# A written instruction order made anew: GpSimd held behind VectorE's integer steps in the first stages, and new lists for the rest

## The chip, the cores and the metric

The kernel runs on one NeuronCore of one Trainium2 chip. The core has a matrix engine (TensorE, PE in the profile), three engines for elementwise work (VectorE = DVE, ScalarE = ACT, GpSimd = POOL) and a sync engine (SP) that here only issues transfers. The metric is the device time of one execution in microseconds (us), lower is better; times are medians over runs.

## The reference

Two blocks, one behind the other. The first is attention through a small set of inducing points: 4 batches of 12,416 rows with 128 channels, 32 inducing rows.

```python
def mab(q, kv):
    s = scale * (q @ kv.transpose(0, 2, 1))
    s = s - s.max(-1, keepdims=True)
    a = np.exp(s)
    a /= a.sum(-1, keepdims=True) + 1e-09
    return a @ kv
h = mab(I, x)                  # 32 rows attend to all of x
attn_out = mab(x, h)           # each row of x attends to the 32 rows h
```

The second takes all 49,664 rows through an RMS norm and a SwiGLU network with an inner width of 1536:

```python
xn = x / np.sqrt(np.mean(x * x, -1, keepdims=True) + 1e-06) * rms_g
g = xn @ w_gate
out = (g / (1.0 + np.exp(-g)) * (xn @ w_val)) @ w_out
```

The three weight matrices arrive as 64-bit floats, and the chip has to make 32-bit floats of them.

## The kernel before, in words

The second attention and the gate and value products are folded together: per batch the kernel computes h, multiplies it into `w_gate` and `w_val`, and keeps the result as stacks `sg` and `sv`. A row of x then needs its 32 normalised attention weights, split into a high and a low half and laid out by four transfers as a moving operand `a` (`gather`, L633 to L647), and one product each with a 128-wide slice of `sg` and `sv`.

**Units and blocks.** A batch has 25 units of up to 512 rows, 100 in all; a unit has 12 blocks, one for each 128 of the inner width. A block is a gate product (L709), a silu on ScalarE (L719), a value product (L737), the product of both on VectorE (L751), and the way through `w_out` to the unit's output bank. That way has three kinds, chosen per block by the letters of the list `sorts`:

- P: one product in plain fp32 (`project_plain`, L807), which reads u and `wo` as they are.
- S: u stays in a PSUM bank; ScalarE makes a high part (L764), VectorE the low part (L770), GpSimd a sum (L815), and TensorE runs three fp32r products (L795, L796, L807).
- D: u lies in SBUF; ScalarE makes the high part (L761, L783), GpSimd the low part and the sum (L777, L815), then the same three products.

So a P costs more on TensorE and less on the other three; S and D spread the other work differently over VectorE, ScalarE and GpSimd.

**What sets the order.** Nothing is scheduled by a compiler: every engine gets its instructions in the order in which the Python code emits them, and semaphores make an engine wait for data. For the first stages, up to the first gate products, the order is the string `ORDER` in `first()`, beside `BANKS`, `WORKERS` and `OUTPUTS` for the buffers. Its words are steps: `t` turns a strip of x by TensorE, `c` copies it out (its last letter is the engine: A, V or G), `s` makes scores, `m` takes them out with their maximum, `e` exponentials, `r` turns them by VectorE, `h` sums. `th` and `hT` end the first attention. Then come, in three parts k = 0, 1, 2 of the first 512 rows, `sc`, `T`, `rm`, `sub`, `ex` (scores, turn, row maximum, subtraction, exponential), `ta`, `sq`, `zm`, `sm`, `mm`, `rt`, `ap` (the norm; `rt` is a power on GpSimd, L1066), `tb`, `hi`, `lo` (the halves), and `sdh`, `sdl`, `sdm`, `cpa`, `cpb`, which lay out the first two units' operands by products with a selection matrix (L1088). `silu` loads ScalarE's table. `w4` are four products of the identity with itself into a bank that nobody reads (`warm`, L158).

Between them stand the steps that make 32-bit weights (`rounding`): for chunk `ic`, `p` and `u` (L231, L244) cut out exponent and mantissa as integers on VectorE, `P` and `U` (L209, L211) turn them into numbers, `g` and `l` (L253, L259) put sign and low word in, `j` (L265) is the product of both parts on GpSimd, `q` sends it off.

After `first()` the rest follows a second set of lists: `program` gives one letter per step, a dot standing for the next of 879 numbered steps in `taken` (strip loads L111, row loads L104, turns, norms, weight steps and so on), and `banks`, `workers`, `outputs`, `holders`, `picks` and `sorts` give each its bank, buffer or kind. Both sets are outputs of a planner that searches with its own costs; only the lists stand in the kernel.

In the loop over `program`, a GpSimd instruction that is emitted next after one of the weight steps `power`, `upper`, `sign` or `lower` gets a wait for that VectorE instruction. `first()` has no such rule.

Strip loads (`load_channels`) bring 32 channels of a later batch's rows each, in short pieces; they go through the same SP queue as the gathers and the stores.

Of the kernel before, what the change touches and what calls it, by code (L numbers as in the profile page):

```python
# [18 lines left out]
P = 128  # L19
# [4 lines left out]
def kernel(  # L24
# [10 lines left out]
    nc = tc.nc  # L35
# [236 lines left out]
    turns, works, outs, factors = [], [], [], []  # L272

# [600 lines left out]
    for s in (1, 2, 0, *range(3, NS)):  # L874
# [8 lines left out]
        0123410234012340123401234012304132041320413024301  # L883
    """
    WORKERS = "012021"
    OUTPUTS = "01010"
    ORDER = """
        open w11 t13 t11 t12 t10 c11A w1 t21 c12A t23 c13V c10V t20 c21A s1 c20V t01 c23V c01A m1 t00 c00A t22 t03 t02
        c22A s2 c02A c03V s0 m2 t31 m0 own0 t33 c31V c33V t43 mB0 nb0 t30 c30V c43A e2 t32 c32V t40 c40V t41 t53 e1 c41A
        r2 t42 r1 t60 c53A p00 u00 e0 t51 c60A c42A ls0 t52 r0 t50 s3 c51A s6 c50A s4 c52A p10 P10A m3 P00A s5 m6 p20  # L890
        P20A h0 m4 m5 own1 mB1 own2 mB2 g00 U00A nb1 l00 e3 nb2 u20 h1 h2 r3 h3 e5 r5 e4 j00 e6 least r4 ls1 h5 ls2
# [10 lines left out]
    def first():  # L902
# [343 lines left out]
    def seams():  # L1246
# [13 lines left out]
        5672340156372450721456701425140571240715420745127450172407512510752317052317024537032407263742746043267304234073  # L1260
        4270327053127305127031251512450126401526140526041245143624532757364735263456735745146517507654107641754055172457
        3571725742135724130725412354615267526471260541072467043764162106714625014725437240732413072103271403716207365127
        6351726513267136364716376471630714306217420761405726450145102614264350264032520754302434750324102475146506267467
        0526470357620165073126507261576507610576501463154634165462526531246534127651675042607456270452706534253761374623
        4726314672312470612764125714257162517462714751467104360146703476014721367306327652062763765230176501201327041270
        2731047230276346734267432643572453670524605246104561462105640216412354362514516521467562317546230152304624254302
        4675204375230170412032731243710421013641263416536253421632451637167457614164501765124705140512521054314523045301
        2754207356047235275204352407310723420473407624073062753046705435637306350160576132751037501347531740537415074316
        5074150714570124502674150415301673107160731531602761057140520645165065241046045314350434145101305147320154703427
        6073657043574657403643517654752732674723546725340673241062703620172610732617036172517602407645067562405764350243  # L1270
# [288 lines left out]
```

## Time and profile before

| | |
|---|---|
| median of 3 runs | 1473.55 us (1472.82 to 1476.4) |
| the profiled execution's own time | 1473.84 us |
| its span in the trace | 1472.1 us |
| busy: PE / DVE / POOL / ACT | 1462.6 / 1427.8 / 1374.5 / 1305.7 us |
| granted TensorE clock, mean | 0.999 |
| first gate product (L709) starts at | 45.05 us |
| PE busy from 64 us to 1467.1 us | 1403.09 of 1403.10 us |
| DVE busy in the same stretch | 1374.70 us |

Times in the trace count from the span's start. A line of the timeline gives start, length, engine, code line, operation, what is written and read, shape and count, and in brackets the idle time before it with what ended it. A name with "ld" (PEld) is a weight load, one with "q" a queue that issues. TensorE's matmuls overlap: a row's length is longer than its distance to the next start, so costs on TensorE are read from distances. A granted clock of 1.00 is full speed, 0.50 half.

### The profile page before, as it was taken

Reading aid. Unit: us, or ns where it says so; the run is one execution under the profiler, and the core shown is the slowest. Engines: PE = TensorE matmul, PEld = TensorE weight load, DVE = VectorE, ACT = ScalarE, POOL = GpSimd, SP = SyncE. Lnnn points to the kernel's source line nnn. Section 1 sums busy time; section 2 is a strip of 40 time slices with the busy share of each in tenths; the row PEclk is TensorE's granted clock in tenths of the full one; section 3 lists DMA queues with packets and bytes.
Section 4 is the critical chain, followed back from the end, with each engine's and each line's share of the span. In section 5 each row is a group of like instructions: output and inputs, shape, how many; then the busy total and the mean of one; then the engine's idle time right before and its main releaser. Section 6 shows DMA issues by size and latency. Waiting matters only on the chain.

```text
span 1472.1 us, 26044 instructions
## 1 busy us (share of the span) xinstructions
PE 1462.6 (99%) x7303; PEld 1105.9 (75%) x7303; DVE 1427.8 (97%) x2483; ACT 1305.7 (89%) x2604; POOL 1374.5 (93%) x1212
## 2 busy tenths in 40 slices
PE   9999999999999999999999999999999999999998
PEld 7566777867777777786777777787777777777787
DVE  7999999999999999999999999999999999999998
ACT  5798899889998889998989898998998899989997
POOL 1499998999999999899999999899999999999998
PEclk9999999999999999999999999999999999999999
DMA  7754323557434131455655212263322112122122
GB/s 282 148 102 101 68 42 75 114 128 137 84 66 87 29 70 39 104 122 107 127 89 108 51 36 47 50 130 94 67 57 47 33 37 44 37 40 40 38 41 35
DMA packets 391904, 116.02 MB, mean 79 GB/s; under 512 B 365648, under 2 KB 371280, under 8 KB 389200
## 3 DMA queue, kind: packets, MB, share of 16 engines
q1 hardware_dynamic: 391168, 114.28, 37.7%
q8 instruction: 58, 0.95, 0.3%
q14 instruction: 86, 0.70, 0.2%
q10 hardware_dynamic: 592, 0.08, 0.0%
HBM read 53.95 MB, written 27.00 MB: 55 GB/s over the span
## 4 chain that ended last, share of the span: by engine, by line
PE 96%; DVE 1%; DMA 1%; issue 0%; SPq 0%; POOL 0%; ACT 0%; DVEq 0%
PE gv L807 32%; PE gv L709 17%; PE gv L737 17%; PE gv L795 12%; PE gv L796 12%; PE gv L316 3%; PE gv L369 1%; DMA xn<-in_x_dram 1%; PE gv L563 1%; PE gv L457 0%; PE gv L978 0%; SPq L104 0%; DVE o L259 0%; DVE u L751 0%; PE gv L934 0%
## 5 line engine op out<-in xcount | busy, mean ns | idle before, releaser
L719 ACT ACTIVATE silu<-gv 128x512 f32<-128x512 f32 (+2 forms) x1200 | 675.0, 591 | 81.1 <-PE gv L709 64.6
L815 POOL TENSOR_TENSOR xn<-xn,xn 128x512 fp32r<-128x512 f32 (+2 forms) x489 | 604.8, 1252 | 15.2 <-PE gv L796 10.3
L709 PE MATMUL gv<-a,sg 128*128 128x512 f32 (+2 forms) x1188 | 481.6, 432 | 0.0
L737 PE MATMUL gv<-a,sv 128*128 128x512 f32 (+2 forms) x1188 | 449.7, 411 | 0.0
L751 DVE TENSOR_TENSOR gv<-silu,gv 128x512 f32<-128x512 f32 (+2 forms) x653 | 429.0, 676 | 7.5 <-ACT silu L719 3.6
L764 ACT ACTIVATE xn<-gv 128x512 fp32r<-128x512 f32 (+1 forms) x630 | 368.7, 597 | 31.9 <-DVE gv L751 26.0
L751 DVE TENSOR_TENSOR u<-silu,gv 128x512 f32<-128x512 f32 (+2 forms) x547 | 347.6, 653 | 7.5 <-PE gv L737 3.9
L807 PE MATMUL gv<-u,wo 128*128 128x512 f32 (+2 forms) x718 | 352.1, 575 | 0.2 <-POOL wo L265 0.2
L770 DVE SCALAR_TENSOR_TENSOR xn<-xn,gv 128x512 fp32r<-128x512 f32 (+2 forms) x508 | 332.0, 664 | 7.1 <-ACT xn L764 4.8
L709 PEld LDWEIGHTS gv<-a,sg 128*128 128x128 f32 x1188 | 224.4, 190 | 100.0 <-issue 30.5
L737 PEld LDWEIGHTS gv<-a,sv 128*128 128x128 f32 x1188 | 223.8, 189 | 90.3 <-issue 21.1
L815 POOL TENSOR_TENSOR xn<-xn 128x512 fp32r<-128x512 f32 (+2 forms) x185 | 232.5, 1260 | 7.5 <-PE gv L796 4.7
L777 POOL TENSOR_TENSOR xn<-u,xn 128x512 fp32r<-128x512 f32 (+2 forms) x166 | 204.5, 1237 | 12.7 <-ACT xn L761 11.4
L815 POOL TENSOR_TENSOR u<-xn,u 128x512 fp32r<-128x512 f32 (+1 forms) x143 | 180.0, 1267 | 0.8 <-PE gv L796 0.7
L795 PE MATMUL gv<-xn,xn 128*128 128x512 f32 (+2 forms) x447 | 169.7, 380 | 0.0
L807 PEld LDWEIGHTS gv<-u,wo 128*128 128x128 f32 x718 | 133.8, 190 | 26.9 <-issue 9.5
L807 PE MATMUL gv<-xn,xn 128*128 128x512 f32 (+2 forms) x372 | 139.5, 386 | 0.0
L796 PE MATMUL gv<-xn,xn 128*128 128x512 f32 (+2 forms) x372 | 139.1, 374 | 0.0
L795 PE MATMUL gv<-xn,more 128*128 128x512 f32 (+2 forms) x341 | 131.3, 385 | 0.0
L761 ACT ACTIVATE xn<-u 128x512 fp32r<-128x512 f32 (+2 forms) x187 | 115.6, 619 | 9.6 <-DVE u L751 8.1
L783 ACT ACTIVATE xn<-xn 128x512 fp32r<-128x512 f32 (+2 forms) x187 | 116.3, 628 | 7.0 <-POOL xn L777 5.8
L807 PE MATMUL gv<-xn,more 128*128 128x512 f32 (+2 forms) x286 | 110.8, 392 | 0.0
(235 smaller groups left out, 1840.5 us busy)
## 6 DMA issues: line engine op xcount, KB each, us to landing
out_dram<-o SPq DMA_DIRECT2D x320, 64.0 KB, 2.0
xT<-in_x_dram SPq DMA_DIRECT2D x60, 256.0 KB, 4.4
xn<-in_x_dram SPq DMA_DIRECT2D x60, 256.0 KB, 5.1
a<-hi SPq DMA_DIRECT2D x152, 64.0 KB, 2.0
a<-lo SPq DMA_DIRECT2D x152, 64.0 KB, 2.0
xn<-in_x_dram SPq DMA_DIRECT2D x5, 1024.0 KB, 9.3
xn<-w SPq DMA_DIRECT2D x18, 256.0 KB, 4.1
out_dram<-o SPq DMA_DIRECT2D x64, 60.0 KB, 2.0
```

The source lines that it names most:

```text
L709: nc.tensor.matmul(g[:, 0:T], stacks[b][0][:, ts(j, P)], halves_in_turn(one["a"][:, 0:T]), start=True, stop=True)
L719: nc.scalar.activation(sl[:, 0:T], gates.pop(n)[:, 0:T], AF.Silu)
L737: nc.tensor.matmul(v[:, 0:T], stacks[b][1][:, ts(j, P)], halves_in_turn(one["a"][:, 0:T]), start=True, stop=True)
L751: nc.vector.tensor_tensor(out=to, in0=sl[:, 0:T], in1=v[:, 0:T], op=ALU.mult)
L764: nc.scalar.activation(hi, t["u"], AF.Copy, scale=-(1.0 - 2.0 ** -13) * 2.0 ** -12)
L770: nc.vector.scalar_tensor_tensor(out=t["lo"], in0=t["hi"].bitcast(F32), scalar=4096.0, in1=t["u"], op0=ALU.mult, op1=ALU.add)
L777: nc.gpsimd.tensor_tensor(out=t["lo"], in0=t["u"], in1=t["hi"].bitcast(F32), op=ALU.subtract)
L783: nc.scalar.activation(t["hi"], t["hi"].bitcast(F32), AF.Copy, scale=-(2.0 ** -12))
L795: nc.tensor.matmul(to, weight_of(0, j), halves_in_turn(t["hi"]), start=not one["q"], stop=False)
L796: nc.tensor.matmul(to, weight_of(1, j), halves_in_turn(t["lo"]), start=False, stop=last)
L807: nc.tensor.matmul(to.rearrange("p (n h) -> p h n", h=2) if step2 else to, lhsT, rhs, start=one["left"] == NJ, stop=one["left"] == 1)
L815: nc.gpsimd.tensor_tensor(out=t["lo"], in0=t["hi"].bitcast(F32), in1=t["lo"].bitcast(F32), op=ALU.add)
```

## The change

Three things are edited.

1. The rule that makes GpSimd wait becomes a function `in_turn`, used by `first()` as well. After a step in `locks` (the integer steps `p`, `u`, `g`, `l`, and those `P`, `U`, `fr` that are given to VectorE), its last instruction is held; the next step that ends in a GpSimd instruction gets a wait on it at its first instruction.
2. `ORDER` and `BANKS` are new. Among other things one strip copy fewer is on VectorE, `sub0` goes from GpSimd to VectorE and `sub2` the other way, `ap1` goes to VectorE, `lo0` and `lo1` go from VectorE to GpSimd, `silu` stands ahead of `hi0`, and the unread products are 23 in all (22 before), eight of them right ahead of `sdh0` and six where eleven stood at the start.
3. All lists of the rest are new. By `sorts` there are 354 P, 662 S and 184 D (359, 653 and 188 before). In rows of 512, 480 and 256, P goes from 267, 71, 21 to 266, 69, 19, and S from 542, 97, 14 to 548, 94, 20. Steps and shapes are otherwise the same.

```diff
+    held = []
+
+    def in_turn(step, args, lock):
+        made = len(nc.cur_bb.bb.instructions)
+        step(*args)
+        new = nc.cur_bb.bb.instructions[made:]
+        if lock:
+            held[:] = new[-1:]
+        elif held and new and new[-1].engine == mybir.EngineType.Pool:
+            tc.add_manual_dep(new[0], held.pop().name, mybir.DependencyInfo(mybir.DependencyClass.Sync, mybir.DependencyReason.DATA),
+                              reason="no two at the shared port")
...
     ORDER = """
...
-        share shared tl r6 g10 spl rl U20A h4 q00 hs0A frA th0 u10 hs1A h6 l20 g20 U10A l10 hs2A th1 th2 hTA w2 sc0 p11
-        hgA sqh gc T0 rm0 sc1 j20 T1 sub0G ex0 rm1 sub1G sc2 T2 ta0 ex1 u11 ta1 st0 sq0 zm0 stc0 U11A q20 j10 q10 P11A
-        sm0 mm0V w1 sq1 rt0 rm2 zm1 sub2V sm1 ex2 mm1V w2 st1 stc1 ap0V tb0 hi0 low0 w4 sdh0 rt1 lo0V low1 sdl0 ap1G
-        sdm0 silu tb1 hi1 cpb0A p01 cpa0V lo1V P01A w1 sdh1 sdm1 sdl1 cpb1A cpa1A u01 U01V
...
+        shared r6 tl p20 p01 hs0A spl P10A hs1A h5 rl frA th0 P20A u20 g10 q00 l10 U20A l20 h6 hs2A g20 th1 w1 th2 hTA
+        w2 sc0 T0 hgA P01A sc1 T1 rm0 sqh j20 gc sc2 rm1 sub1G sub0V T2 ex0 ta0 ex1 ta1 st0 rm2 j10 w1 sq0 stc0 zm0 sm0
+        sub2G mm0V sq1 ex2 zm1 rt0 sm1 mm1V low0 ap0V tb0 silu hi0 rt1 ap1V st1 stc1 tb1 lo0G hi1 w8 sdh0 q20 w1 sdl0
+        p11 sdm0 lo1G cpa0A sdh1 low1 cpb0A P11A w1 sdm1 u01 u11 q10 cpb1A U01V sdl1 cpa1A U11V
     """
...
+        locks = {f"{key}{i}{c}{by}" for i, c in chunks for key, by in (*zip("pugl", ("",) * 4), ("P", "V"), ("U", "V"))} | {"frV"}
         for name in ORDER.split():
-            do[name]()
+            in_turn(do[name], (), name in locks)
...
-    held = None
     alone = {id(one[name]) for one in weight.values() for name in ("power", "upper", "sign", "lower")}
     for name in "".join(program.split()):
-        made = len(nc.cur_bb.bb.instructions)
         step, args = micros[int(next(taken))] if name == "." else (do[name], ())
-        step(*args)
-        one = nc.cur_bb.bb.instructions[-1]
-        if id(step) in alone:
-            held = one
-        elif held is not None and one.engine == mybir.EngineType.Pool and len(nc.cur_bb.bb.instructions) > made:
-            tc.add_manual_dep(one, held.name, mybir.DependencyInfo(mybir.DependencyClass.Sync, mybir.DependencyReason.DATA),
-                              reason="no two at the shared port")
-            held = None
+        in_turn(step, args, id(step) in alone)
```

More of the change, by code (lines that the diff above doesn't have):

```diff
@@ L1284 @@
-        2407563240762347017
+        5674130256174302653024631602314062310426304162403164026143614302614076214076241036421635260135215603251032512034
+        5704571042751407523071207310273610276037231627361237013125317247315472150732457125321627536751671236153076513750
+        7453451401743052173021735203105705635761760345701547341725702754751047624752370250240542764207560274602174603241
+        0217413720546130173051354731703105340571245743673741534367317451267345173461540635613465036154025360432473604727
@@ L1285 @@
+        3241063247012640162
     """
     workers = """
-        20120201201201022012102210210211212012100120120102012012020120120
+        20120102102102010120120201201201201201212120120102011021010210210
     """
@@ new lines @@
+        AAAAAAAAAAAAABAAAAAABAABAAAAAAABAAAAAAAAAABAACAACABAAAAAABABAAAAAAABAAAAAAAAAAAAAAAAAAAABAAAAAAAABAAAAAAAABAAAAA
+        ABAAAAAABAAAAAAAAABAAAAABAAAAABAAAAAAAAABAAAAABAAAAAAABAAAAAAAAAAAAAAAAAAAAAAAAAAAAABAAAAAAAAAABAAAAABAAAAAAAAAA
+        AABAAAAAAABAAAAAAABABAAABABBAAABAAAAAAAAAACAAAAAAAAAAAAAAAAAAABAAAAAAAAAAABAAAAAAAAAAAAAAAAABAAAAAAAAAAAAAABAAAA
+        AAAAAAAAAAAAABAAAAAAABAAAAAAAAABABAAAAAAAAAAAAAAAAAAAAAAAAAAAAAAAAAAAAAAAAAAAAAAAAAABAAAAAAABAAAABAAAAAABAAAAAAA
+        AAAAABAAAAAAAAABAAAAAAAAAAAAAAAAAAAAAAAAABAAAAAAABAAAAABAAABAAAA
```

395 lines of the change are left out of this document (193 added, 202 removed), and 60 rows, old and new, of the table taken.

## The prediction

> **What bounds the kernel now.** I read the totals first, then busy time by stretch, then TensorE's waits.
>
> ```profile
> span 1472.1 us, 26044 instructions
> PE 1462.6 (99%) x7303; PEld 1105.9 (75%) x7303; DVE 1427.8 (97%) x2483; ACT 1305.7 (89%) x2604; POOL 1374.5 (93%) x1212
> ```
> ```profile
> core 0: us, PE busy (x) PEld busy (x) DVE busy (x) ACT busy (x) POOL busy (x), PEclk, DMA share, GB/s
> 38.38:41.79 3.41, 3.03 (x18) 2.32 (x18) 3.24 (x12) 2.77 (x6) 2.15 (x3) 1.00 0.84 245
> 41.79:45.20 3.41, 2.57 (x18) 2.14 (x18) 3.26 (x9) 2.59 (x6) 0.30 (x1) 1.00 1.05 166
> 45.20:48.62 3.42, 3.42 (x13) 2.21 (x15) 3.42 (x7) 2.76 (x7) 0.27 (x2) 0.50 0.34 55
> 48.62:64.00 15.38, 15.19 (x54) 7.58 (x55) 13.77 (x26) 10.07 (x19) 7.56 (x6) 1.00 0.81 162
> 64.00:1467.10 1403.10, 1403.09 (x6772) 1064.72 (x6770) 1374.70 (x2351) 1266.45 (x2520) 1355.89 (x1179) 1.00 0.36 72
> ```
> ```profile
> PE gv L158 <- POOL ident masks.py:199: 1.3, 1, 1.3
> ...
> PE gv L807 <- POOL wo L265: 0.2, 1, 0.2
> ```
>
> From 64 us to the last product TensorE is never idle, and VectorE is idle for 28.4 us of 1403.1. The list of TensorE's waits has six rows that add up to 4.2 us (first and last shown), and all lie ahead of 64 us. So a change can pay in two ways: the first 45 us, whose length goes straight into the end, or less work on TensorE. A stall behind 64 us can hardly be removed, but it can be added. The third row of the stretches is the odd one: for 3.42 us the granted clock is 0.50, right where the first gate products run.
>
> **The first stages, the wait at GpSimd.** The timeline shows what the new wait is aimed at:
>
> ```profile
> 31.39 0.41 DVE L244 TENSOR_SCALAR o<-sc 128x512 int32<-128x512 int32 x1
> 31.71 0.68 DVE L259 SCALAR_TENSOR_TENSOR o<-sc,o 128x512 f32<-128x512 uint32 x1
> 33.07 1.27 POOL L265 TENSOR_TENSOR wo<-o,we 128x512 f32<-128x512 f32 x1 [3.80 <-DVE we L253]
> 33.10 1.79 DVE L259 SCALAR_TENSOR_TENSOR o<-sc,o 128x512 f32<-128x512 uint32 x1
> 36.75 1.27 POOL L265 TENSOR_TENSOR silu<-o,we 128x512 f32<-128x512 f32 x1
> 36.93 1.37 DVE L244 TENSOR_SCALAR o<-sv 128x512 int32<-128x512 int32 x1
> ```
>
> The same steps take 0.68 and 0.41 us alone, 1.79 and 1.37 us when a GpSimd product started just ahead of them. So two collisions hold VectorE for 1.11 and 0.96 us. What stands behind them:
>
> ```profile
> 34.24 0.43 PE L1025 MATMUL gv<-xT,hT 128*32 128x128 f32 x8
> 35.15 0.30 DVE L1028 STREAM_TRANSPOSE sc<-gv 128x128 f32<-128x128 f32 x1
> 37.06 0.49 PE L1049 MATMUL gv<-eT,gram 128*128 128x128 f32 x2 [0.21 <-DVE eT L1045]
> 38.45 0.25 DVE L1053 TENSOR_TENSOR eT<-gv,eT 128x128 f32<-128x128 f32 x1
> 39.33 1.04 POOL L1066 TENSOR_TENSOR rs<-ms,mhalf 128x4 f32<-128x4 f32 x1 [1.31 <-DVE ms L1062]
> 41.09 0.69 DVE L486 TENSOR_TENSOR sg<-gv,sg 64x512 fp32r<-64x512 f32 x1
> 41.09 0.30 ACT L1078 CAST hi<-eT 128x128 fp32r<-128x128 f32 x1
> 41.41 1.28 ACT L1107 ACT_TABLE_LOAD   x1
> 41.82 0.42 DVE L1084 TENSOR_TENSOR lo<-eT,hi 128x128 fp32r<-128x128 f32 x1
> 43.34 0.30 ACT L1078 CAST hi<-eT 128x128 fp32r<-128x128 f32 x1 [0.43 <-DVE eT L1073]
> 45.05 1.00 PE L709 MATMUL gv<-a,sg 128*128 128x512 f32 x2
> ```
>
> - *First turn of scores (35.15).* The scores are there at 34.67, and the turn waits for VectorE: at least 0.4 us comes back. One strip copy fewer and one earlier `r` take up to 0.7 us more off VectorE, but other chains feed hT as well: 0 to 1.1, and I take **0.6**, the near end being what the row shows.
> - *From that turn to the power (39.33), 4.18 us.* The square is done at 37.55, and its product (38.45) sits behind the stretched step of 36.93: 0.85 back. The new order puts `sub0` on VectorE behind T1, rm0 and rm1, and a weight step (0.73) more on ScalarE ahead of `ex0`: 0.2 given. Net 0.65.
> - *Power to second half (43.34).* `low0` (0.69) no longer stands between `hi0` and `lo0`; `ap1` and `tb1` no longer wait behind L486. Against it, the table load (1.28) is now ahead of `hi0`; laid out with these lengths it ends 0.3 us too late. The wait brings one cost of its own: `lo1` on GpSimd is held by `p11` on VectorE (L231, 0.4 us), of which 0.3 lies beside `hi1`. Laid end to end, the first gate product comes 8.1 us behind the first turn where it came 9.9 us behind it. The sum of small steps is sure only by half, so 0.6 to 2.4, and I take **1.7**.
>
> Queued behind GpSimd's new waits are only `sub1` and `sub2` (L1036): each join in question needs a late integer step of its own anyway. Six unread products where eleven stood lengthen nothing; they run while the first strips land.
>
> **The clock.** Eight products run in the stretch at 0.50. Two distances from later, at full speed, and the cost of a plain product:
>
> ```profile
> 607.47 0.38 PE L795 MATMUL gv<-xn,more 128*128 128x512 f32 x1
> 607.68 0.38 PE L796 MATMUL gv<-xn,more 128*128 128x512 f32 x1
> 608.55 1.02 PE L807 MATMUL gv<-u,wo 128*128 128x512 f32 x2
> 609.62 0.38 PE L795 MATMUL gv<-xn,xn 128*128 128x512 f32 x1
> ```
>
> A full-speed fp32r product takes 0.215 us, so half speed costs 3.42/2 = 1.7 us. It follows 3.41 us with little on TensorE (sixteen selections at about 0.06 and four unread passes, some 1.1 us, though its row says 2.57, since lengths overlap). The new order puts eight unread products (two passes at 0.11 each: 1.75 us) into that gap. The 38.38 stretch, with 3.03 in its row, was not followed by a slow one. A gap with 1.75 us of passes more should resemble it: I take **1.7**; the ends are 0 and 1.7, since I don't know what fill suffices.
>
> By the Trainium skill, TensorE: Matmul & The Clock Gate (The HAM clock gate), the watch window of some 3.4 us runs freely and does not start with the kernel; the 3.41 us here agree. By that rule the order cannot place the window, and this term would be 0 or 1.7 by chance.
>
> **TensorE's work behind that.** Between 608.55 and 609.62 stand one plain product and one value product of 0.215: a P is 0.86, three fp32r products are 0.65. Five P less and five triples more: 512 rows 1 × 0.21, 480 rows 2 × 0.20, 256 rows 2 × 0.11, so **0.8** off.
>
> ```profile
> L770 DVE SCALAR_TENSOR_TENSOR xn<-xn,gv 128x512 fp32r<-128x512 f32 (+2 forms) x508 | 332.0, 664 | 7.1 <-ACT xn L764 4.8
> ```
>
> Nine S more (by length 6, −3, 6) put 6 × 0.66 − 3 × 0.62 + 6 × 0.4, about 4.5 us, on VectorE; its 28.4 us of idle time hide it, at nothing. With that cover gone it is 4.5.
>
> **The new lists.** TensorE's order is as dense, so I take 0 for stalls; the ends: −3 (no more than the few tenths between rows could give) and, above, late gathers:
>
> ```profile
> 110.44 0.57 SPq L647 DMA_DIRECT2D a<-hi  x1
> 112.96 0.58 SPq L647 DMA_DIRECT2D a<-lo  x1
> 115.20 0.59 PE L709 MATMUL gv<-a,sg 128*128 128x512 f32 x2
> DMA to landing us min/median/max: 2.0/2.3/3.2
> xT<-in_x_dram SPq DMA_DIRECT2D x60, 256.0 KB, 4.4
> ```
>
> The fourth transfer of this gather, issued at 112.96, lands at 114.96 at best, 0.24 us ahead of the gate product that reads it. Strip loads take 4.4 where a gather takes about 2. A rule that lets gathers behind them come later cannot gain where nothing waits; it can only keep such a margin.
>
> **Sum.** 0.6 + 1.7 + 1.7 + 0.8 = 4.8 off the profiled execution's 1473.84 (its span 1472.1 and 1.7 around it): 1469.0. That execution was 0.3 above the median, which gives 1468.7; I say 1468.9.
>
> **The rivals.**
>
> - *The slow window comes all the same*, elsewhere or in the same place: 1468.9 + 1.7 = 1470.6. For it: I don't know the fill that suffices.
> - *The earlier start is eaten.* VectorE still has weight steps between 48.62 and 64 us, and it is busy for 13.77 of 15.38 us there, a tenth from full; if those steps hold the first units, the 2.3 us of the first stages are lost, and with the clock unhealed all but 0.8: 1471 to 1473. Against it: the row still has 1.6 us free.
> - *The shared path hits other steps.* A GpSimd join slows not just integer steps: `sub0` on VectorE now runs beside one, and the rest of that join, up to 1.1 us, lies on the chain: 1470.0. The near row speaks against it: at 39.68 a subtraction with two inputs in SBUF ran 0.41 us beside the power on GpSimd, though that moves little.
>
> ```profile
> 39.68 0.41 DVE L1036 TENSOR_TENSOR sc<-sc,mx 128x256 f32<-128x256 f32 x1
> ```
>
> The Trainium skill, GPSIMD Engine Reference (Key points), speaks for it: GpSimd contends with VectorE instructions that have two SBUF inputs, which the new wait does not cover.
>
> - *The wait does nothing*, as steps emitted later still meet a running join: the 1.4 us for collisions (0.4 + 0.96) stay, 1470.3.
> - *Slower: gathers come late.* In the new order a gather stands behind strip loads at a place where the margin was 0.24 us. One strip ahead costs 0.6 at issue and up to 2.4 in landing, 3 us, all of it TensorE idle. Gains of 4.8 cover one such place; from four on the kernel is slower by more than 0.3% (1468.9 + 12 = 1480.9). Against it: only a few of 98 gathers are that tight, and a search that prices strips moves away from them.
>
> **Chances.** A measurement tells about 0.3% (4.4 us) from no change. The full sum or more: 0.47, below 1469.1. Window, shared path, no effect or eaten start (1470 to 1473.5) and small stalls: 0.38, within 0.3%. Late gathers or another stall that the rows can't show: 0.15. The range goes from 1463.8 (first stages 3.5 instead of 2.3, stalls −3, some tenths more) to 1478 (three late gathers). The likeliest case alone: 1466 to 1469.5.
>
> **What would show it.** Right: the first gate product near 42.5 us; L259 and L244 at 0.68 and 0.41 throughout; no stretch at 0.50 behind 5 us; TensorE still without idle time behind 64 us. Wrong: rows of TensorE waiting for transfers, for VectorE or for ScalarE behind 64 us, a stretch at 0.50 beside the first gates, or a first gate product at 44 us or later.

## The result and the profile after

| | before | after |
|---|---|---|
| median of 12 runs each | 1473.89 us (1472.56 to 1476.4) | 1470.41 us (1469.96 to 1471.29) |
| ratio, 95% interval | | 0.9974 (0.9966 to 0.9983) |
| the profiled execution's own time | 1473.84 us | 1469.96 us |
| span | 1472.1 us | 1468.1 us |
| first gate product | 45.05 us | 41.52 us |
| end of the last product | 1467.10 us | 1463.14 us |
| from the one to the other | 1422.05 us | 1421.62 us |

The changed kernel is 3.5 us faster by the medians (2.5 to 5.0 by the interval), about a quarter of a per cent: inside the range given, 1.5 us behind the forecast, and smaller than the 0.3% (4.4 us) that the prediction took a measurement to need, though this interval lies clear of no change. The size is less sure than the sign: repeated in a later group of runs, the medians differ by 2.7 us (experiment 11), for the kernel before scatters from 1472.5 to 1476.9 us over the study, the changed one from 1469.9 to 1472.1. Three executions are left out of these ranges and of the ratios, two of the kernel before (4122 and 6146 us) and one of experiment 8 (3974 us); the record shows no cause for them. The profiled execution of the changed kernel is one of the two shortest of its twelve, 0.45 us below the median.

In the changed kernel the code lines from L273 of the kernel before on are higher by 11: the gate product L709 is now L720, the value product L737 is L748, L751 is L762, L807 is L818, L1028 is L1039, L1088 is L1099. The lines of the weight steps (L231 to L265) are the same.

The totals of the changed kernel and the engines' shares of the chain of work that ended last, and then those shares for the kernel before:

```profile
span 1468.1 us, 26087 instructions
PE 1460.1 (99%) x7310; PEld 1106.3 (75%) x7310; DVE 1427.4 (97%) x2489; ACT 1304.2 (89%) x2607; POOL 1376.3 (94%) x1214
...
PE 98%; DVE 1%; ACT 0%; issue 0%; POOL 0%; POOLq 0%; DVEq 0%; ACTq 0%
```
```profile
PE 96%; DVE 1%; DMA 1%; issue 0%; SPq 0%; POOL 0%; ACT 0%; DVEq 0%
```

Before, a transfer stood on the chain that ends last, with 1% of the span. These are not the first strips of x but late ones: a load issued at 4.10 us that lands at 20.02, and in front of two turns TensorE waits for such strips (the first line is of the chain, the others of the timeline of the kernel before):

```profile
4.10 15.92 DMA xn<-in_x_dram
17.28 0.66 PE L934 MATMUL gv<-ident,xn 128*128 128x128 f32 x4 [0.42 <-DMA xn<-in_x_dram]
20.16 1.06 PE L934 MATMUL gv<-ident,xn 128*128 128x128 f32 x8 [0.30 <-DMA xn<-in_x_dram]
```

In the changed kernel TensorE waits for no strip, and the chain is TensorE's alone but for 1% of VectorE.

The changed kernel's busy time by stretch (engines in the order PE, PEld, DVE, ACT, POOL, then the granted clock), and its waits of TensorE, all three rows of them:

```profile
core 0: us, PE busy (x) PEld busy (x) DVE busy (x) ACT busy (x) POOL busy (x), PEclk, DMA share, GB/s
33.13:41.00 7.87, 7.50 (x60) 5.71 (x52) 7.24 (x23) 5.78 (x17) 6.02 (x8) 1.00 0.84 225
41.00:64.00 23.00, 21.81 (x77) 12.05 (x75) 22.81 (x44) 18.11 (x33) 10.06 (x9) 1.00 0.68 137
64.00:1463.10 1399.10, 1398.98 (x6770) 1063.36 (x6768) 1373.70 (x2352) 1259.94 (x2513) 1354.94 (x1179) 1.00 0.37 72
```
```profile
PE gv L158 <- POOL ident masks.py:199: 1.3, 1, 1.3
PE gv L818 <- DVE u L762: 1.0, 1, 1.0
PE gv L1099 <- ACT hi L1089: 0.4, 1, 0.4
```

The clock is 1.00 in all of these stretches; the one at 0.50 beside the first gate products is gone. Behind 64 us TensorE is busy for 1398.98 of 1399.10 us. A new row stands in the list of waits: the first plain product waits 1.0 us for u. The stretch from 41 to 64 us has VectorE busy for 22.81 of 23.00 us; before, the same stretch reads

```profile
41.00:64.00 23.00, 21.79 (x83) 12.30 (x82) 21.20 (x42) 16.12 (x32) 8.84 (x9) 0.93 0.79 151
```

The timeline of the changed kernel at the places of the prediction:

```profile
4.87 1.60 PE L158 MATMUL gv<-ident 128*128 128x128 f32 x12
6.31 1.91 PE L945 MATMUL gv<-ident,xn 128*128 128x128 f32 x16
...
30.59 1.45 DVE L259 SCALAR_TENSOR_TENSOR o<-sc,o 128x512 f32<-128x512 uint32 x2
32.72 1.28 POOL L265 TENSOR_TENSOR wo<-o,we 128x512 f32<-128x512 f32 x1 [4.07 <-DVE we L253]
33.13 0.53 DVE L1039 STREAM_TRANSPOSE sc<-gv 128x128 f32<-128x128 f32 x2 [0.49 <-PE gv L1036]
33.94 0.28 DVE L1047 TENSOR_TENSOR sc<-sc,mx 128x128 f32<-128x128 f32 x1
36.82 1.95 PE L158 MATMUL gv<-ident 128*128 128x128 f32 x16
38.79 0.30 ACT L1089 CAST hi<-eT 128x128 fp32r<-128x128 f32 x1 [0.45 <-DVE eT L1084]
41.52 0.65 PE L720 MATMUL gv<-a,sg 128*128 128x512 f32 x2
44.48 0.68 DVE L259 SCALAR_TENSOR_TENSOR o<-sv,o 128x512 f32<-128x512 uint32 x1
45.19 1.88 DVE L762 TENSOR_TENSOR u<-silu,gv 128x512 f32<-128x512 f32 x3
45.93 1.13 PE L818 MATMUL gv<-u,wo 128*128 128x512 f32 x2 [1.04 <-DVE u L762]
```

The first strip is turned at 6.31 (7.21 before), the first turn of scores comes at 33.13 (35.15) and the first gate product at 41.52 (45.05). Where VectorE came late to the first turn of scores, it now waits 0.49 us for the scores. L259 has 1.45 us for two, no stretched one. The sixteen passes at 36.82 are the eight unread products. At the end of the list the weight step of 44.48 stands ahead of the product u of 45.19, and TensorE waits 1.04 us for it.

### The profile page after: what moved, and what is told of

Same layout as the page of the kernel before. It is cut to its first block, busy times and chain, and to the rows that moved or that the text cites. A ratio compares the mean times of both kernels' runs of the same rounds, so it can differ in the third digit from the quotient of the medians.

```text
span 1468.1 us, 26087 instructions
## 1 busy us (share of the span) xinstructions
PE 1460.1 (99%) x7310; PEld 1106.3 (75%) x7310; DVE 1427.4 (97%) x2489; ACT 1304.2 (89%) x2607; POOL 1376.3 (94%) x1214
## 4 chain that ended last, share of the span: by engine, by line
PE 98%; DVE 1%; ACT 0%; issue 0%; POOL 0%; POOLq 0%; DVEq 0%; ACTq 0%
PE gv L818 32%; PE gv L720 17%; PE gv L748 17%; PE gv L806 12%; PE gv L807 12%; PE gv L327 3%; PE gv L380 1%; PE gv L945 1%; PE gv L574 1%; PE gv L158 0%; PE gv L989 0%; PE gv L468 0%; DVE u L762 0%; ACT silu L730 0%; PE gv L1099 0%
## 5 line engine op out<-in xcount | busy, mean ns | idle before, releaser
L826 POOL TENSOR_TENSOR xn<-xn,xn 128x512 fp32r<-128x512 f32 (+2 forms) x468 | 580.7, 1257 | 23.0 <-PE gv L807 20.7
L720 PE MATMUL gv<-a,sg 128*128 128x512 f32 (+2 forms) x1188 | 478.4, 432 | 0.0
L748 PE MATMUL gv<-a,sv 128*128 128x512 f32 (+2 forms) x1188 | 449.4, 411 | 0.0
L762 DVE TENSOR_TENSOR gv<-silu,gv 128x512 f32<-128x512 f32 (+2 forms) x662 | 432.6, 673 | 6.1 <-PE gv L748 2.9
L775 ACT ACTIVATE xn<-gv 128x512 fp32r<-128x512 f32 (+2 forms) x643 | 376.2, 596 | 34.9 <-DVE gv L762 28.3
L762 DVE TENSOR_TENSOR u<-silu,gv 128x512 f32<-128x512 f32 (+2 forms) x538 | 343.1, 655 | 7.6 <-ACT silu L730 3.8
L818 PE MATMUL gv<-u,wo 128*128 128x512 f32 (+2 forms) x708 | 347.8, 577 | 1.2 <-DVE u L762 1.0
L720 PEld LDWEIGHTS gv<-a,sg 128*128 128x128 f32 x1188 | 223.4, 189 | 102.2 <-issue 33.2
L748 PEld LDWEIGHTS gv<-a,sv 128*128 128x128 f32 x1188 | 223.0, 189 | 85.4 <-issue 23.1
L826 POOL TENSOR_TENSOR xn<-xn 128x512 fp32r<-128x512 f32 (+2 forms) x200 | 250.8, 1261 | 6.5 <-PE gv L807 6.2
L788 POOL TENSOR_TENSOR xn<-u,xn 128x512 fp32r<-128x512 f32 (+2 forms) x159 | 197.4, 1245 | 7.9 <-ACT xn L772 6.3
L826 POOL TENSOR_TENSOR u<-xn,u 128x512 fp32r<-128x512 f32 (+2 forms) x154 | 194.4, 1271 | 1.9 <-PE gv L807 1.7
L806 PE MATMUL gv<-xn,xn 128*128 128x512 f32 (+2 forms) x451 | 170.2, 378 | 0.0
L818 PEld LDWEIGHTS gv<-u,wo 128*128 128x128 f32 x708 | 132.0, 190 | 30.0 <-issue 12.0
L818 PE MATMUL gv<-xn,xn 128*128 128x512 f32 (+2 forms) x360 | 134.9, 385 | 0.0
L807 PE MATMUL gv<-xn,xn 128*128 128x512 f32 (+2 forms) x360 | 134.5, 374 | 0.0
L772 ACT ACTIVATE xn<-u 128x512 fp32r<-128x512 f32 (+2 forms) x179 | 110.8, 620 | 9.2 <-DVE u L762 8.4
L794 ACT ACTIVATE xn<-xn 128x512 fp32r<-128x512 f32 (+2 forms) x179 | 112.1, 629 | 4.6 <-POOL xn L788 3.3
L818 PE MATMUL gv<-xn,more 128*128 128x512 f32 (+2 forms) x292 | 112.4, 393 | 0.0
```

The costliest lines, as they stand in the source:

```text
L720: nc.tensor.matmul(g[:, 0:T], stacks[b][0][:, ts(j, P)], halves_in_turn(one["a"][:, 0:T]), start=True, stop=True)
L748: nc.tensor.matmul(v[:, 0:T], stacks[b][1][:, ts(j, P)], halves_in_turn(one["a"][:, 0:T]), start=True, stop=True)
L762: nc.vector.tensor_tensor(out=to, in0=sl[:, 0:T], in1=v[:, 0:T], op=ALU.mult)
L775: nc.scalar.activation(hi, t["u"], AF.Copy, scale=-(1.0 - 2.0 ** -13) * 2.0 ** -12)
L788: nc.gpsimd.tensor_tensor(out=t["lo"], in0=t["u"], in1=t["hi"].bitcast(F32), op=ALU.subtract)
L794: nc.scalar.activation(t["hi"], t["hi"].bitcast(F32), AF.Copy, scale=-(2.0 ** -12))
```

## The experiments

Since the kernel before scatters, ratios are given with the kernel before of the same group. The next table holds, from each profile, the times that the theories speak of: *strip* is the first turn of a strip, *scores* the first turn of scores, *gate* the first gate product, *end* the end of the last product, all in us; *clock* is when the clock first reads 1.00. Each row is one execution. The last column can move by about 1 us from one to the next at a place far behind all edits: at about 664 us the weight loads of L468 wait for a transfer, 1.1 us in early_m, 0.6 in no_w8, 0.5 in join_first, 0.3 in numbers_act and not at all in again, no_lock and both. So *join_first* and *both*, with the same lists, differ by 0.62. Whether the edits have a part in this wait is not shown.

| kernel | clock | strip | scores | strip to scores | gate | scores to gate | gate to end |
|---|---|---|---|---|---|---|---|
| before | 4.2 | 7.21 | 35.15 | 27.94 | 45.05 | 9.90 | 1422.05 |
| old_w6 | 7.1 | 7.35 | 34.85 | 27.50 | 44.88 | 10.03 | 1422.24 |
| old_w12 | 6.5 | 8.18 | 35.28 | 27.10 | 45.19 | 9.91 | 1421.16 |
| lock_only | 6.8 | 8.34 | 35.01 | 26.67 | 44.38 | 9.37 | 1422.29 |
| after | 4.8 | 6.31 | 33.13 | 26.82 | 41.52 | 8.39 | 1421.62 |
| again | 6.0 | 6.82 | 33.63 | 26.81 | 42.03 | 8.40 | 1421.68 |
| old_lists | 5.4 | 6.55 | 33.36 | 26.81 | 41.74 | 8.38 | 1422.55 |
| no_lock | 7.4 | 7.50 | 34.31 | 26.81 | 42.69 | 8.38 | 1421.73 |
| no_w8 | 6.5 | 7.09 | 33.91 | 26.82 | 43.77 | 9.86 | 1422.94 |
| early_m | 5.1 | 6.42 | 33.23 | 26.81 | 41.62 | 8.39 | 1423.10 |
| join_first | 5.8 | 6.75 | 33.57 | 26.82 | 41.96 | 8.39 | 1422.23 |
| w2 | 6.9 | 5.88 | 33.20 | 27.32 | 41.60 | 8.40 | 1421.59 |
| both | 4.2 | 5.74 | 32.94 | 27.20 | 41.33 | 8.39 | 1421.61 |
| numbers_act | 6.9 | 7.28 | 34.10 | 26.82 | 42.48 | 8.38 | 1421.72 |

**1. The new first stages with the old lists.**

```diff
-    banks, workers, outputs, holders, sorts, picks, program, taken = (the new lists)
+    banks, workers, outputs, holders, sorts, picks, program, taken = (the lists of before)
```

> First stages of the changed kernel (with the wait), the lists behind them from before. If the gain lies in the first stages: first gate product at 41.5 us, no stretch at 0.50 beside it, and 3.5 + 1.7 - some stalls less than before: 1469 to 1470.5 us, so as fast as the changed kernel or faster by up to 1. If the old lists do not fit the new start (the rival that the earlier start is eaten): first gate product at 41.5 us all the same, but TensorE waits behind it, and 1471 to 1474 us.

Measured: 1471.39 us (1470.67 to 1472.12), ratio to before 0.9987 (0.9978 to 0.9996). From the first gate product to the end 1422.55 us, 0.93 more than in the changed kernel; the medians differ by 0.98. Against experiment 2, which ran in the same group with the new lists, it is 0.63. So the new lists bring some 0.6 to 1.0 us and the first stages the rest: 1.8 us against the kernel before of this group (1473.17), 2.5 by the medians of the result. The time is that of the second theory (1471 to 1474), and TensorE does wait behind the gate: 0.6 us for u and 0.4 for `wo`. But not all of the 0.93 is TensorE's work. Against the profile of experiment 5, with the same lists, the same silu on ScalarE is 2.86 us ahead at 75 us and the last one only 2.06; these 0.8 us are lost far behind, and why was not looked into. The five P less were put at 0.8. The reverse exchange, the old first stages with the new lists, was not run.

**2. The changed kernel without the new wait.**

```diff
         for name in ORDER.split():
-            in_turn(do[name], (), name in locks)
+            in_turn(do[name], (), False)
```

> The changed kernel, without the new wait in the first stages. If the wait is what removes the collisions: one or two of L231, L244, L253, L259 stretched to 1.4 to 1.8 us between 30 and 42 us, first gate product 0.5 to 1.5 us later than 41.5 us, 0.5 to 1.5 us more than the changed kernel. If the new order alone keeps the steps apart: all at 0.4 and 0.7 us, first gate product at 41.5 us, same time as the changed kernel.

Measured: 1470.76 us (1469.8 to 1471.3), ratio 0.9978 (0.997 to 0.9987). That is the second theory, the new order alone. The timeline without the wait:

```profile
4.87 2.80 PE L158 MATMUL gv<-ident 128*128 128x128 f32 x12
...
31.76 1.46 DVE L259 SCALAR_TENSOR_TENSOR o<-sc,o 128x512 f32<-128x512 uint32 x2
33.90 1.28 POOL L265 TENSOR_TENSOR wo<-o,we 128x512 f32<-128x512 f32 x1 [4.08 <-DVE we L253]
34.31 0.53 DVE L1039 STREAM_TRANSPOSE sc<-gv 128x128 f32<-128x128 f32 x2 [0.49 <-PE gv L1036]
```

No integer step is stretched here either: two L259 take 1.46 us and the join starts behind them. From the first strip to the scores it is 26.81 us, from there to the gate 8.38, as with the wait. In the new order the wait changes nothing; the order of the words alone keeps the join and the integer steps apart. All of this run is later by 1.19 us, because the same twelve passes end 1.2 us later (2.80 for 1.60): the clock came to full speed at 7.4 us and not at 4.8.

**3. The kernel before, with the wait alone.**

```diff
         for name in ORDER.split():
-            do[name]()
+            in_turn(do[name], (), name in locks)
```

> The kernel before with the new wait in the first stages, nothing else. If collisions were worth what the prediction took for them (0.4 ahead of the first turn, 0.85 behind it): L259 at 0.68 and L244 at 0.42 us, first gate product at 43.8 us, 1.2 us less than before. If the wait turns into lateness of GpSimd's own steps on the chain (subtractions behind the joins): first gate product at 44.5 us or later, no gain or up to 1 us more.

Measured: 1473.32 us (1471.83 to 1473.64), ratio 0.9998 (0.9989 to 1.0006). Its timeline:

```profile
31.98 0.69 DVE L259 SCALAR_TENSOR_TENSOR o<-sc,o 128x512 f32<-128x512 uint32 x1
33.37 0.69 DVE L259 SCALAR_TENSOR_TENSOR o<-sc,o 128x512 f32<-128x512 uint32 x1
34.48 1.27 POOL L265 TENSOR_TENSOR wo<-o,we 128x512 f32<-128x512 f32 x1 [4.69 <-DVE we L231]
35.01 0.32 DVE L1039 STREAM_TRANSPOSE sc<-gv 128x128 f32<-128x128 f32 x1 [0.61 <-PE gv L1036]
36.81 0.39 DVE L244 TENSOR_SCALAR o<-sv 128x512 int32<-128x512 int32 x1
37.28 1.27 POOL L265 TENSOR_TENSOR silu<-o,we 128x512 f32<-128x512 f32 x1 [0.46 <-DVE o L244]
```

Here the wait does what it says. Both joins stand behind the step that they had stretched, L259 takes 0.69 for 1.79 and L244 0.39 for 1.37. But the 2.1 us of VectorE's time become little: from strip to scores 26.67 where a kernel of before with the same start of strips (old_w12) has 27.10, so 0.43, and from scores to gate 9.37 for 9.90, so 0.53. The first gate product is 0.5 to 0.8 earlier than in the three rows of the old order, the end 0.4 earlier than in those with the slow stretch, and the median shows none of it. The gate's 44.38 falls between the two theories (43.8, or 44.5 and later). What the eleven executions do show is less scatter: none takes over 1473.7 us, where 13 of 33 of the kernel before in this group take over 1474.

**4. The changed kernel without the eight unread products.**

```diff
-        ... stc1 tb1 lo0G hi1 w8 sdh0 q20 w1 sdl0
+        ... stc1 tb1 lo0G hi1 sdh0 q20 w1 sdl0
```

> The changed kernel without the eight unread products ahead of the selections. If they keep the clock up: a stretch of 3.4 us at 0.50 behind 38 us, up to 1.7 us more than the changed kernel in the profiled execution and 0.5 to 1.7 us in the median. If the slow window was a matter of where it fell: granted clock 1.00 from 5 us on, and the same time as the changed kernel, with at most 0.3 us either way from the products themselves.

Measured: 1473.11 us (1472.0 to 1473.76), ratio 0.9991 (0.9982 to 1.0). The stretches of this kernel, 3.4 us each:

```profile
core 0: us, PE busy (x) PEld busy (x) DVE busy (x) ACT busy (x) POOL busy (x), PEclk, DMA share, GB/s
33.90:37.30 3.40, 3.40 (x28) 1.93 (x20) 3.03 (x12) 2.27 (x9) 3.10 (x4) 1.00 0.51 154
37.30:40.70 3.40, 1.25 (x8) 0.77 (x7) 3.19 (x10) 2.79 (x6) 2.48 (x3) 0.99 0.94 262
40.70:44.10 3.40, 3.40 (x17) 3.40 (x17) 3.33 (x7) 1.83 (x5) 0.46 (x1) 0.50 1.07 168
44.10:47.50 3.40, 3.40 (x9) 2.67 (x9) 3.25 (x7) 2.62 (x6) 1.44 (x2) 0.50 0.21 32
```

A stretch with 1.25 us of TensorE work is followed by 6.8 us at 0.50. In the new order eight products of 128 columns are thus worth 2.6 us (1473.11 against 1470.41 and 1470.53), more than either theory had. This is not the fill's share of the change: the kernel before had four such products ahead of its first selections, and one slow stretch in its profile where this one has two. The price is paid behind the gap: the selections ahead of the gate run at half speed too (scores to gate 9.86 for 8.39). That the second slow stretch came although the first was full of work, the runs don't explain.

**5. The kernel before with twelve unread products in place of four.**

```diff
-        ... ap0V tb0 hi0 low0 w4 sdh0 rt1 ...
+        ... ap0V tb0 hi0 low0 w12 sdh0 rt1 ...
```

> The kernel before with twelve unread products instead of four ahead of the first selections. If fill keeps the clock up: no stretch at 0.50 behind 5 us, first gate product 0 to 0.9 us later (eight products take 1.75 us, part of it in idle time), and 0.8 to 1.7 us less than before. If where the window falls decides: a stretch at 0.50 in some executions as before, and the same time as before or up to 0.9 us more.

Measured: 1472.93 us (1472.62 to 1473.71), ratio 0.9992 (0.9983 to 1.0001). Its stretches:

```profile
45.30:48.60 3.30, 3.30 (x25) 1.68 (x24) 3.30 (x6) 3.06 (x7) 0.21 (x2) 1.00 0.49 78
48.60:64.00 15.40, 14.94 (x46) 7.86 (x43) 15.26 (x29) 10.90 (x20) 7.77 (x7) 1.00 0.86 171
```

The fill takes the slow stretch away in the old order as well, and costs nothing ahead of the gate (scores to gate 9.91 for 9.90). Of the 1.7 us that the stretch costs, 0.9 to 1.1 reach the end (gate to end 1421.16 for 1422.05 and 1422.24). The second row shows what stands beside it: VectorE is now busy for 15.26 of 15.40 us, where it was 13.77 of 15.38 with the slow stretch ahead.

By the medians of this group the fill brings 0.3 us, which the interval doesn't tell from nothing. The scatter says more. Over the groups, 33 of 106 executions of the kernel before have a mean granted clock of 0.997 or 0.998, and these are the ones that take 1474.8 to 1476.9 us; all others, at 0.999 or 1.000, take 1472.5 to 1474.4. One stretch of 3.42 us at 0.50 takes 0.0012 off the mean, so an estimate is that the low ones have two (the kernel of experiment 4, with two, reads 0.997 in ten of eleven). With the fill all eleven executions read 0.999 or 1.000 and lie within 1.1 us. No profile of the kernel before was taken in an execution of the low kind, so what its 3 us consist of stays open. In the changed kernel none of 23 executions reads below 0.999.

**6. The kernel before with six unread products at the start.**

```diff
-        open w11 t13 t11 t12 ...
+        open w6 t13 t11 t12 ...
```

> The kernel before with six unread products instead of eleven at the start. If those products stood in the way of the first strip (landed at 6.03 us, turned from 7.10 us): first turn of a strip at 6.2 us, and first turn of scores up to 0.9 us ahead of 35.15 us if this carries on. If the last strips' transfers set the pace up to 20 us: first turn of a strip at 6.2 us, first turn of scores at 35.15 us within 0.2, and no change in time.

Measured: 1474.01 us (1472.45 to 1475.83), ratio 0.9997 (0.9988 to 1.0006). In the old order the five products fewer bring the scores 0.3 us ahead (34.85) and the time nothing that can be told. Both theories had the strip turned at 6.2 us, and it was turned at 7.35: the clock came to full speed only at 7.1, and the twelve passes of the six products (4.87 to 7.52) ran mostly at half speed. Next to *old_w12*, with eleven products and a like start of the clock (6.5), the strip is 0.83 earlier and the scores 0.43.

**7. The changed kernel with two at the start.**

```diff
-        open w6 t12 c12A ...
+        open w2 t12 c12A ...
```

> The changed kernel with two unread products instead of six ahead of the first strip. If these products stand in the way of the first strip: its turn starts at 5.9 to 6.3 us whatever the clock's window, the first turn of scores 26.8 us behind it, and 0.3 to 1.0 us less than the changed kernel in the median. If the last strips or the colder clock set the pace instead: the first turn of scores stays at 33.1 to 34.3 us, and the time does not move by more than 0.3 us.

Measured: 1470.42 us (1469.9 to 1471.08), ratio 0.9978 (0.9969 to 0.9986), the time of the second theory. The first strip is turned at 5.88, but the scores come at 33.20: from strip to scores it is now 27.32 and no longer 26.82. The first line below is of this run, the second of the run `both` (experiment 9), which has two products as well:

```profile
5.88 2.41 PE L945 MATMUL gv<-ident,xn 128*128 128x128 f32 x16
5.74 1.97 PE L945 MATMUL gv<-ident,xn 128*128 128x128 f32 x16 [0.40 <-DMA xn<-in_x_dram]
```

With the clock at full speed only from 6.9 us, the first sixteen turns take 2.41 us for the 1.91 of the changed kernel, and that is the 0.5 us. With the clock at 1.00 from 4.2, TensorE waits 0.40 us for the strip instead. Six are few enough.

**8. The first product of u earlier.** In the list of the rest, the first product u (L762) stands behind five weight steps on VectorE. It was put ahead of the last two of them:

```diff
     program:
-        .gg.vs.vg.sgvs.gv.g......m.mspms.
+        .gg.vs.vg.sgvs.gv.gm.......mspms.
```

> The changed kernel with the first product of silu and value (L762) moved ahead of the weight steps power 1,2 and lower 1,1 on VectorE. If the 1.3 us that TensorE loses at 44.9 us are VectorE's weight steps standing ahead of that product: the wait at the first plain product goes (under 0.3 us), and 0.9 to 1.3 us less than the changed kernel. If the weight steps are what bounds the first units: the wait moves to a later product that needs the weights, and the time stays within 0.4 us of the changed kernel.

Measured: 1470.91 us (1470.09 to 1471.55), ratio 0.998 (0.9971 to 0.9989). The wait for u is gone from the list of TensorE's waits and another has come:

```profile
PE gv L490 <- POOL xn L265: 1.3, 1, 1.3
PE gv L468 <- DMA out_dram<-o: 0.2, 1, 0.2
```

The product L490 reads the weights that the delayed weight steps make. The time is that of the second theory: the median is 0.4 to 0.5 above the changed kernel's. Gate to end is 1423.10 in the profiled execution, 1.5 more than without this edit, but only about 0.4 of that arises near it; the other 1.1 us are those of the second row, at 664 us.

**9. The join first, two products u beside it, and then the other weight steps.**

```diff
     program:
-        .gg.vs.vg.sgvs.gv.g......m.mspms.
+        .gg.vs.vg.sgvs.gv.g...mm....spms.
     taken:
-        62 24 88 115 5 87 25 2 3
+        62 88 115 2 24 5 87 25 3
```

> The changed kernel with the join of chunk 0,1 right behind its last integer step, the first two products of silu and value on VectorE beside it, and power 1,2, lower 1,1 and the clearing of the next Gram matrix behind those. If the 1.3 us that TensorE loses ahead of the first plain product come from this join's and product's places (the join held behind lower 1,1, which it does not read): the join starts at 44.2 instead of 45.4 us, neither the first plain product nor the first product with chunk 0,1 waits over 0.4 us, and 0.9 to 1.3 us less than the changed kernel. If the weight steps as a whole bound the first units: the loss comes back at chunk 1,1 (at 50 to 53 us), and the time is within 0.4 us of the changed kernel.

Measured: 1470.55 us (1470.07 to 1471.01), ratio 0.9975 (0.9967 to 0.9984). The same with two unread products at the start:

> Both edits at once. If the two are independent: the sum of their gains, 1.2 to 2.3 us less than the changed kernel. If the first units are bound by the weight steps: no more than the one gain at the start, if that.

Measured: 1470.54 us (1469.76 to 1470.87), ratio 0.9979 (0.997 to 0.9988): neither edit brought any of the gain that the first theories had. I summed, over TensorE's rows from 41 to 64 us, what each distance between two ends exceeds the usual one for that shape (the median of its kind; excesses over 0.1 us). In the changed kernel that is 2.05 us, of which 1.31 lie at the first plain product. In these two kernels it is 2.03 and 2.03, in pieces of 0.3 to 0.5 at five places. The wait was split and not shortened.

**10. Two number steps from VectorE to ScalarE.** This is to tell whether VectorE's being full is the cause.

```diff
-        ... u01 u11 q10 cpb1A U01V sdl1 cpa1A U11V
+        ... u01 u11 q10 cpb1A sdl1 cpa1A U01A U11A
```

> The changed kernel with the two number steps U0 and U1 of chunk 1 (two VectorE instructions of 0.38 us each, right ahead of the weight steps that hold the first products of unit 0) moved to ScalarE, at the end of the first stages. The order on TensorE and GpSimd stays.
>
> Theory A (what is lost behind the first gate product is VectorE being full between 41 and 64 us, 22.81 of 23.00): VectorE has 0.76 us less to do there, so the sum of TensorE's lost time between 41 and 64 us falls from 2.0 us to about 1.3 to 1.6, the wait for u at the first plain product from 1.0 to about 0.3 to 0.6, the distance from first gate product to last product from 1421.6 to about 1421.0, and the time from 1470.4 to about 1469.8.
>
> Theory B (a fixed amount is lost whatever VectorE does, because GpSimd's joins or ScalarE's silus set the pace): the wait for u shrinks but the loss appears elsewhere, sum still about 2.0, distance 1421.6, time 1470.4; if ScalarE's two steps (0.62 each) delay the first silus beyond what VectorE gains, 1470.8 to 1471.2.

Measured: 1470.43 us (1469.7 to 1471.0), ratio 0.9978 (0.9969 to 0.9987). VectorE is busy for 22.34 us for 22.81:

```profile
41.00:64.00 23.00, 22.46 (x82) 12.46 (x82) 22.34 (x41) 19.14 (x36) 9.57 (x10) 1.00 0.73 144
```
```profile
42.59 0.82 DVE L253 SCALAR_TENSOR_TENSOR we<-sv,we 128x512 int32<-128x512 int32 x1 [0.20 <-ACT we L209]
43.66 0.83 DVE L259 SCALAR_TENSOR_TENSOR o<-sg,o 128x512 f32<-128x512 uint32 x1 [0.24 <-ACT o L211]
44.68 0.48 PE L748 MATMUL gv<-a,sv 128*128 128x512 f32 x1 [0.26 <-ACT silu L730]
```

The freed time goes into VectorE's waits for ScalarE, the first u starts 3.64 us behind the gate product (3.67 in the changed kernel), and TensorE's excess is 1.92 for 2.05. So the theory of a full VectorE, taken alone, is not borne out: giving it less to do brought nothing, and the rows show ScalarE holding it then. What is shown is that three ways to move this work (experiments 8, 9 and 10) leave about 2 us lost or more. Whether the making of these weights as a chain over three engines sets that, or something else, stays open.

**11. The changed kernel once more, unedited,** on the same chip as experiments 7 and 9:

> The changed kernel once more, unedited, as the one that the next three are compared with on the same chip: 1469.9 to 1471.3 us as in its twelve runs, first turn of scores 26.8 us behind the first turn of a strip, first gate product 8.4 us behind that.

Measured: 1470.53 us (1469.94 to 1472.12), ratio 0.998 (0.9971 to 0.9989). No kernel of the study beats the changed one by anything that can be told.

## Why the prediction was right, and which terms were not

The forecast was 1468.9 and the result 1470.4, with the sign right and inside the range. The case called likeliest (1466 to 1469.5, at 0.47) did not come; 1470.4 lies in the band of 1470 to 1473.5 that was given 0.38 for rivals that come true. The forecast's sum was 4.8 us. By the profiles it looks like this:

| term | predicted | measured |
|---|---|---|
| first turn of scores | 0.6 | 2.0 (35.15 to 33.13; 1.5 with again's 33.63) |
| from there to the first gate product | 1.7 | 1.5 (9.90 to 8.39) |
| the clock | 1.7 | 1.7 of slow stretch gone |
| TensorE's work behind | 0.8 | at most 0.9 (1422.55 to 1421.62) |
| what is gained kept to the end | all | less about 2 |
| sum | 4.8 | 4.0 (1467.10 to 1463.14) |

That 4.0 came out near 4.8 is in part luck: the first term was 1.4 us too small, about 2 us of loss stood in no term, and the two nearly cancel.

*The first turn of scores.* The term was mis-sized, beyond its own upper end of 1.1, and one sentence shows why: "Six unread products where eleven stood lengthen nothing; they run while the first strips land." It put at nothing what was a gain. The first strip had landed at 6.03 (issued at 0.72, 5.3 us to landing) and was turned at 7.21 behind the eleven; with six it is turned at 6.31. That is 0.9 of the 2.0 us, and the rest lies between strip and scores. There the kernel before waits 0.7 us for late strips (17.28 and 20.16 above), and the changed one doesn't. In the old order an early first turn runs into those strips: with the strip at 7.21 it is 27.94 us to the scores, with the strip at 8.18 and no such wait 27.10. So experiment 6 found little (0.3 to 0.4 us), and it is the new order of the strips that can use the earlier start. What this is worth also depends on the execution: with six products, the first gate product comes at 41.52 us when the clock is full from 4.8 and at 42.69 when it is full from 7.4. The profiled execution of the changed kernel has the earliest such start of all runs with six.

*The wait.* The mechanism was right for the old order, and its size was not. Undoing the collisions gave 0.43 and 0.53 us (experiment 3) where 0.4 and 0.85 were taken, and the median of that kernel moved by nothing that can be told, though its scatter shrank. In the new order the wait is idle, as experiment 2 shows. That is the rival "the wait does nothing" with another reason: it isn't that later steps meet a running join, but that no join meets a step even without the wait. The 1.5 us from scores to gate belong to the new order of the chain.

*The shared path at other steps* was hardly put to the test: `sub0` on VectorE started at 33.94, and the join of 32.72 ended at 34.00. What did run beside joins in the changed kernel kept its usual length: the transposes of 33.13 (0.53 for two) and the products u of 45.19, which read the bank `gv` (three in 1.88). No larger step on floats with both inputs in SBUF ran beside a join for longer than these 0.06 us.

*The clock.* Right that the fill keeps the clock up, and a large part: without it the changed kernel takes 2.6 us more (experiment 4). The fill of 1.75 us was enough in every profile of the new order, at starts of the clock from 4.2 to 7.4 us. By the Trainium skill, TensorE: Matmul & The Clock Gate (The HAM clock gate), the watch window of about 3.4 us runs freely; that the same kernel comes to full speed at 4.8 us in one execution and 6.0 in another agrees. The inference that the order then cannot place the gain was the part that failed: with this much work in the gap the phase no longer mattered in any profile taken. For the kernel before, where executions differ in their mean clock, it may well hold. The page has half speed follow an idle window; here it followed one with 1.25 us of work in 3.40, and the measurement decides. How much fill suffices is not read from a row's busy time. In the kernel before 2.57 us in a stretch were followed by half speed; in the changed kernel (the first two rows) and in early_m (the third) less was not:

```profile
42.40:45.80 3.40, 2.49 (x15) 1.11 (x14) 3.37 (x7) 2.45 (x5) 0.58 (x2) 1.00 0.68 106
45.80:49.20 3.40, 3.27 (x9) 1.78 (x10) 3.40 (x8) 3.23 (x6) 1.52 (x2) 1.00 0.35 102
46.09:49.50 3.41, 2.11 (x7) 1.21 (x7) 3.08 (x7) 3.26 (x7) 1.90 (x3) 1.00 0.31 90
```

In early_m too the clock stays at 1.00 behind it. The prediction's own count for the kernel before, some 1.1 us, is not safe either: it takes a selection at 0.06 and gives 1.4 when its counts are summed, and in the rows selections start 0.11 us apart (42.57, 42.68 and 42.79). The stretches differ in what runs, mostly selections of 128 columns in the kernel before and products of 512 in these two, but no run separates this.

*TensorE's work behind.* Of the right order: 0.8 predicted; the 0.9 of experiment 1 holds up to 0.8 us that its profile lost elsewhere, so the runs neither fix this size nor speak against it. VectorE's 4.5 us more stayed hidden behind 64 us. The risk that was priced highest for a slower kernel, gathers behind strip loads, did not come: no wait for a gather stands in the list of waits (the late transfer at 664 us in some of the other profiles brings weights), and behind 64 us TensorE is short of 0.12 us of its time.

*What failed* is that the terms were added up as if they all reached the end. The rival "the earlier start is eaten" came true in part: of some 6 us gained, about 2 were lost again behind the first gate product, 1.31 of it at the first plain product, 0.28 and 0.41 at two places up to 60 us. The prediction had read a sign of it, VectorE busy for 13.77 of 15.38 us from 48.62 on, and set it aside because 1.6 us were free. That free time stood beside a stretch of TensorE at half speed; with the clock at full there was hardly any in the old order too (15.26 of 15.40, experiment 5). VectorE's load alone is not the cause (experiment 10); the chain that holds the first units stays open. The rival's price of 2.3 us is near this loss; that a gain was left is due to first stages that brought 3.5 us and not 2.3.

## What to carry to other kernels

Slack that is read beside a slow stretch need not be there when the stretch is cured: of two gains in a row, take the second one's cover from a profile in which the first is already made. A short stretch in which TensorE has little to do can cost more behind it than in it, and a few unread products in the gap are a cheap cure; here they held in every phase met. Before a difference between two profiles is put down to an edit, look where in the run it arises: one of 1.5 us came for the most part from a late transfer 600 us behind the edit. A wait against a collision is worth only what the order doesn't already do; try the new order without it before crediting it.

## What the runs showed of the hardware that was not expected

- The same kernel reaches the full clock at 4.8 or 6.0 us (after and its repetition), over all kernels between 4.2 and 7.4. With six products at the start, the first gate product of the new order moves by a little under half of that (1.17 us for 2.55).
- A gap with 1.25 us of TensorE work in 3.40 us was followed by two slow stretches, 6.8 us in all, though TensorE had work throughout the first of them; a gap with about 2.6 us in its row (kernel before) was followed by one, gaps with 2.49 (changed kernel) and 2.11 (early_m) by none.
- A GpSimd product that starts 0.03 us ahead of a VectorE step with an integer input stretched that step from 0.68 to 1.79 us; when the product starts behind the step, neither is longer than alone (0.69 and 1.27). Transposes (0.53 for two) and products that read a PSUM bank (1.88 for three) were not stretched beside such a product.
- In the kernel before the executions with a mean granted clock of 0.997 or 0.998 are the ones over 1474.8 us (33 of 106); with twelve unread products in the gap there was none in eleven.
